# Seven products for eight in the first matmul of an fp32 MLP beside attention, with the second matmul's banks added to the output by transfers

## The chip, the core and the metric

The kernel runs on one core of a Trainium2 chip. The core has five engines with their own in-order instruction streams: TensorE (PE; matmuls from SBUF into PSUM), VectorE (DVE), ScalarE (ACT), GpSimd (POOL) and SyncE (SP, which mainly issues DMA transfers). They meet only at semaphores. The metric is the device time of one execution in microseconds; lower is better.

## What is computed

The input x is 2048 rows of 576 numbers in float32. It is normalised per row, and two branches take the result xn:

```
xn  = layernorm(x)
qkv = xn @ wqkv                      # 576 x 1728, 32 heads of 18
A   = softmax over 8 keys (positions s, s-2, ... s-14) of q.k, times v, then @ wo
B   = relu(xn @ w1) @ w2             # w1 576 x 4608, w2 4608 x 576
out = x + A + B
```

All is float32. Each large matmul is done with operands cut into a high and a low part (`hi` rounded to the matmul's fast float32 form, `lo` the rest), as hi*hi + hi*lo + lo*hi, so every product costs three matmuls on PE.

## The kernel before, in words

**Tiles.** Rows are taken in two phases (`ph`) of 1024 rows. A phase has 4 token blocks of 256 rows (`tb`), each of two tiles of 128 rows. F = 4608 is 36 tiles of 128 (`f`), in 12 chunks of 3. D = 576 is 4 K tiles of 128 and a rest of 64.

**Slots.** The main loop runs over slots, one for each phase, chunk, token block and F tile: 288 of them. In a slot the *second* product (`o_two`) multiplies the relu'd tile of that slot by w2 into four PSUM banks (two row tiles by the column halves 0:256 and 256:576), and the *first* product (`h_two`) makes two slots' tiles ahead, over two slots. After the third F tile of a chunk, `o_out` (line 765) adds the four banks to the running sum x in SBUF by DVE. After a phase's last chunk the sums are stored.

**Half rows.** Nearly all matmuls use 64 of the 128 rows of the array. `mm_rows` (line 137 of the profile) issues them in pairs, one on the lower and one on the upper 64 rows, which run together into different banks. A tile's first product is 27 such halves: 12 on the lower and 12 on the upper rows (3 hi/lo terms by 4 K tiles), and 3 for the 64 rest rows. Where a bank goes from lower to upper rows PE waits for the last matmul into it.

**First product's output.** ACT writes the high part with relu (line 651), DVE the low part (line 654).

**Attention.** Four units of 8 heads per phase. QKV for a unit runs in 8 slots; the attention itself is a list of DVE instructions (`bg`: multiply, reduce, softmax, multiply, add in halves) that `run_bg` pours into the gaps. It keeps an estimate of PE's and DVE's time (`t`) and lets DVE run at most a margin past PE. In chunk 10 the output projection wo joins the second product's banks; attention's output is turned to K-major either through PE (`turn_rows`, line 369) or by DVE's 32x32 transpose and a trip through DRAM (`blocks_out`, `words_in`).

**Weights.** SP loads tiles of w1, w2, wqkv, wo into staging buffers four tasks ahead; ACT makes `hi` (line 170) and DVE `lo` (line 174), POOL in the kernel's head (line 172).

Of the kernel before, what the change touches and what calls it, by code (L numbers as in the profile page):

```python
# [3 lines left out]

# [14 lines left out]
P = 128  # L19
# [7 lines left out]
C = 3  # L27
LAG = 2
ROW0 = 8
EPS = 1e-5  # L30

UNIT0, UNIT_STEP = (10, 10), 24
WO_CHUNK = 10


XT_STEPS = (
    (-6, -1, 0, 1, 2, 4, 6), (-5, 0, 2, 3, 4, 7, 8), (-3, 2, 4, 5, 6, 8, 9), (4, 6, 7, 10),
    (4, 6, 8, 12), (7, 9, 11, 13), (8, 12, 13, 15), (10, 13, 14, 16),
)

TURN_STEPS = ((-10, -9, -7, -4), (-7, -5, -3, -1), (-4, -3, 0, 1), (-2, 0, 1, 2))
WO_STEPS = (-2, -1)
# [13 lines left out]


@with_exitstack
def tile_body(ctx: ExitStack, tc: tile.TileContext, x, wqkv, wo, w1, w2, out):
# [6 lines left out]
    NCH = NF // C  # L66
# [7 lines left out]
    SPP = NCH * SPC  # L74
# [4 lines left out]

    def space(name, words):  # L80


        pool(name, 1).tile([P, words], F32, name=name)

    consts = pool("consts", 1)
    xp = pool("xp", 11)
    xtp = pool("xtp", NTB)
    qop = pool("qop", 1)
    kp = pool("kp", 1)
    vp = pool("vp", 2)  # L90
    w1p = pool("w1p", C + 1)
    space("gap_w2", 48)
    w2p = pool("w2p", C + 1)
    space("gap_wq", 16)
    wqp = pool("wqp", 1)
    stp = pool("stp", 5)
    hp = pool("hp", LAG + 1)
    prp = pool("prp", 2)
    lgp = pool("lgp", 1)
    smp = pool("smp", 2)  # L100
    space("gap_tmp", 16)
    tmp = pool("tmp", 2)
    turned = pool("turned", 4, space=bass.MemoryType.DRAM)
# [19 lines left out]

    t = {"pe": 0.0, "dve": 0.0}

# [3 lines left out]

    def mm_rows(runs, behind=None):  # L130


        if behind is not None:
            tc.add_manual_dep(nc.tensor.nop().ins, behind.ins.name, SYNC, reason="PSUM banks change rows")
        for pair in zip(*runs, strict=True):
            for z, (o, l, r, start, stop, n) in zip((slice(0, 64), slice(64, P)), pair):
                ins = nc.tensor.matmul(o, l[z], r[z], start=start, stop=stop)  # L137
            t["pe"] += pair[0][5] * 17 / 16 / 2400.0 + 0.001
        return ins

    def dve(n):
        t["dve"] += (n + 70) / 960.0

# [8 lines left out]
    def stage_more(ahead=None):  # L152
        while tasks and len(staged) < (ahead or AHEAD["n"]):
            step, load, split = tasks.popleft()
            st = stp.tile([P, 640], F32, name="st")
            load(st)
            staged.append((step, split, st))
# [11 lines left out]
    def two(hi, lo, src, n):  # L169
        nc.scalar.activation(hi, src, AF.Copy)  # L170
        if step_now in by_pool:
# [7 lines left out]
    def w1_task(step, key, f):  # L179
# [9 lines left out]
        def split(st):  # L189
            w = w1p.tile([P, 2, 5 * P], F32R, name="w1t")  # L190
            two(w[:, 0, :], w[:, 1, :], st[:, :], 640)
            W1[key] = w
# [3 lines left out]
    def w2_task(step, key, f):  # L196
# [3 lines left out]
        def split(st):  # L200
            w = w2p.tile([P, 2, 640], F32R, name="w2t")
            for z, c in zip(W2CUT, CUT):
                two(w[:, 0, z], w[:, 1, z], st[:, c], c.stop - c.start)
# [4 lines left out]
    def wq_tasks(steps, key, g):  # L208
        src = wqkv.rearrange("r (s c) -> r s c", s=3)

        def one(kt):
            def load(st):
                v = st[:, 0 : 3 * UD].rearrange("p (s c) -> p s c", s=3)
                c = slice(g * UD, (g + 1) * UD)
                if kt < KT:
                    nc.sync.dma_start(v, src[kt * P : (kt + 1) * P, :, c])
                else:
                    nc.sync.dma_start(v[0:DR], src[KT * P : D, :, c])
                    nc.sync.dma_start(v[DR:P], src[KT * P : D, :, c])

            def split(st):
                if kt == 0:
                    z = wqp.tile([P, WQ0 + 10 * WQS], F32R, name="wq")[:, WQ0:]
                    WQ[key] = z.rearrange("p (k c) -> p k c", c=WQS)[:, :, 0 : 3 * UD]
                w = WQ[key]
                two(w[:, kt, :], w[:, 5 + kt, :], st[:, 0 : 3 * UD], 3 * UD)

            return load, split

        for kt, step in enumerate(steps):  # L230
            split_task(step, *one(kt))

    def wo_tasks(steps, key):
        def one(kt):
            def load(st):
                if kt < KT:
                    nc.sync.dma_start(st[:, 0:D], wo[kt * P : (kt + 1) * P, :])
                else:
                    nc.sync.dma_start(st[0:DR, 0:D], wo[KT * P : D, :])
                    nc.sync.dma_start(st[DR:P, 0:D], wo[KT * P : D, :])  # L240

            def split(st):
                if kt == 0:
                    a = wqp.tile([P, 7, D], F32R, name="wq")
                    b = vp.tile([P, 3, D], F32R, name="v")
                    WO[key] = [a[:, k, :] for k in range(7)] + [b[:, k, :] for k in range(3)]
                w = WO[key]
                two(w[kt], w[5 + kt], st[:, 0:D], D)

            return load, split  # L250

        for kt, step in enumerate(steps):
            split_task(step, *one(kt))


    X, XT, XN, MR = {}, {}, {}, {}

    def load_x(ph, i):
        if (ph, i) not in X:
            X[ph, i] = xp.tile([P, D], F32, name="x")  # L260
# [7 lines left out]
    def stats(ph, i, parts=False, act=False):  # L268
        xt = X[ph, i]
# [22 lines left out]

    def norm(ph, i, act=False):
        nm, r = MR.pop((ph, i))
        xw = tmp.tile([P, 640], F32, name="xn", bufs=3)
        xn = xw[:, 0:D]
# [6 lines left out]
        if ph:  # L303
            nc.scalar.activation(xw[:, D:640], xn[:, KT * P : D], AF.Copy)
        XN[ph, i] = xw if ph else xn
# [35 lines left out]
    def make_xt(ph, i, bank=None, parts=False):  # L341
# [3 lines left out]
        d = XT[ph, tb][:, :, h * P : (h + 1) * P]  # L345
# [3 lines left out]
    def make_xt_rows(ph, i):  # L349
        tb, h = divmod(i, 2)  # L350
        if h == 0:
            XT[ph, tb] = xtp.tile([P, 10, TBN], F32R, name="xT")
        for c, pt in turn_rows(XN.pop((ph, i))):
            d = XT[ph, tb][:, :, h * P + c : h * P + c + 64]
            nc.scalar.activation(d[:, 5:10], pt, AF.Copy)
            nc.scalar.activation(d[0:DR, 4], pt[0:DR, KT], AF.Copy)
            nc.vector.tensor_tensor(d[:, 0:4], pt[:, 0:KT], f32(d[:, 5:9]), op=ALU.subtract)
            nc.vector.tensor_tensor(d[DR:P, 4], pt[DR:P, KT], f32(d[DR:P, 9]), op=ALU.subtract)
            dve(256)
            dve(64)  # L360

    def turn_rows(src):


        z = [(c, ps_m.tile([P, 5, 64], F32, name="pm")) for c in (0, 64)]
        for k in range(5):
            for c, pt in z:
                rows = slice(c, c + 64)
                nc.tensor.transpose(pt[:, k], src[rows, k * P : (k + 1) * P], ident[rows, rows])  # L369
        t["pe"] += 5 * 0.06  # L370
        return z

    def blocks_out(ph, i):
        td, tr = TD[ph, i]
        for r in range(4):
            rows = slice(32 * r, 32 * r + 32)
            nc.sync.dma_start(
                td[:, :, rows].rearrange("g j i -> j g i"),
                tr[rows, :].rearrange("j (g i) -> j g i", i=32),
# [606 lines left out]
```

## Time and profile before

| | |
|---|---|
| median of 2 runs | 1144.19 us (1143.83 to 1144.56) |
| span of the profiled execution | 1141.6 us; its time with what lies around the span is not listed apart, the median of the runs is 2.6 us over the span |
| PE busy | 1134.5 us, 99% of the span |
| DVE busy | 802.1 us, 70% |
| ACT busy | 303.0 us, 27% |
| POOL busy | 57.1 us, 5% |
| DMA | 83.60 MB, mean 73 GB/s |

The profile's page gives, per engine, the time in which it was executing, and then the chain of work that ended last: from the last instruction back, at each step, to what released it. Groups of instructions are listed as line, engine, operation, output<-inputs, shapes and count, then busy time and the mean of one, then the idle time of the engine just before them and what ended it. "64*128 64x256" on a matmul is 64 rows by 128 columns of weights with 256 moving columns. Matmuls overlap in the pipeline, so a single matmul's duration (273 ns) is longer than the distance from one pair to the next.

### The profile page before, as it was taken

How to read it: one execution, taken by the hardware profiler on the slowest of the kernel's cores; microseconds unless marked ns; L12 is line 12 of the kernel's file. 1: busy time of each engine (PE TensorE's matmuls, PEld its weight loads, DVE VectorE, ACT ScalarE, POOL GpSimd, SP SyncE). 2: the span in 40 equal slices, each digit the busy share in tenths (PEclk: the TensorE clock that was granted, in tenths of full speed). 3: DMA queues.
4: the chain of work that ended last, by engine and by line, in shares of the span. 5: the costliest groups of instructions: out<-in, count | busy, mean ns of one | idle time of the engine just before them, and what ended most of it. 6: DMA issues, size and time to landing. Idle time of an engine off the chain costs nothing.

```text
span 1141.6 us, 38695 instructions
## 1 busy us (share of the span) xinstructions
PE 1134.5 (99%) x17224; PEld 1128.4 (99%) x17224; DVE 802.1 (70%) x1522; ACT 303.0 (27%) x854; POOL 57.1 (5%) x84
## 2 busy tenths in 40 slices
PE   8999999999999999999999999999999999999998
PEld 8999999999999999999999999999999999999998
DVE  7415886887788689854674179868868887896433
ACT  4412222222232212322462122222222312222110
POOL 2400000000000000000110000000000000010000
PEclk9999999999999999999999999999999999999999
DMA  6303212130330312622633033032221304136002
GB/s 192 109 2 94 71 47 67 48 98 6 97 98 13 104 33 50 175 57 63 157 122 98 2 101 88 23 85 63 63 59 47 107 2 114 45 81 152 13 2 84
DMA packets 118855, 83.60 MB, mean 73 GB/s; under 512 B 33201, under 2 KB 102449, under 8 KB 118689
## 3 DMA queue, kind: packets, MB, share of 16 engines
q1 hardware_dynamic: 118256, 80.67, 25.6%
q8 instruction: 135, 2.21, 0.8%
q10 hardware_dynamic: 432, 0.46, 0.1%
q14 instruction: 32, 0.25, 0.1%
HBM read 64.95 MB, written 7.96 MB: 64 GB/s over the span
## 4 chain that ended last, share of the span: by engine, by line
PE 96%; issue 2%; DVE 1%; ACT 0%; DMA 0%; DVEq 0%; POOL 0%; ACTq 0%
PE po L137 41%; PE pm L137 28%; PE ph L137 24%; PE ph L127 1%; PE po L127 1%; PE pm L317 0%; DVE pr L544 0%; DMA x<-in_x 0%; PE pm L369 0%; DVE xn L613 0%; PE pm L127 0%; DVE hlo L654 0%; DVE x L765 0%; ACT xT L322 0%; DVE xn L614 0%
## 5 line engine op out<-in xcount | busy, mean ns | idle before, releaser
L137 PE MATMUL po<-w2t,hhi 64*128 64x256 f32 (+1 forms) x4448 | 444.8, 290 | 0.0
L137 PEld LDWEIGHTS po<-w2t,hhi 64*128 64x128 f32 x4448 | 356.1, 184 | 0.6
L137 PE MATMUL po<-w2t,hlo 64*128 64x256 f32 (+1 forms) x2224 | 331.2, 287 | 0.0
L137 PE MATMUL ph<-xT,w1t 64*128 64x256 f32 x4806 | 305.5, 273 | 0.3 <-DVE hlo L654 0.2
L137 PEld LDWEIGHTS ph<-xT,w1t 64*128 64x128 f32 x4806 | 293.7, 184 | 1.5 <-DVE hlo L654 1.1
L765 DVE TENSOR_TENSOR x<-po,x 128x320 f32<-128x320 f32 (+1 forms) x384 | 149.6, 449 | 149.4 <-PE po L137 146.8
L137 PEld LDWEIGHTS po<-w2t,hlo 64*128 64x128 f32 x2224 | 217.2, 184 | 0.0
L651 ACT ACTIVATE hhi<-ph 128x256 fp32r<-128x256 f32 x187 | 62.1, 382 | 496.8 <-PE ph L137 484.6
L137 PE MATMUL pm<-wq,xT 64*128 64x432 f32 x1728 | 178.8, 354 | 0.0
L137 PE MATMUL pm<-xT,w1t 64*128 64x256 f32 x2700 | 170.6, 273 | 0.0
L137 PEld LDWEIGHTS pm<-xT,w1t 64*128 64x128 f32 x2700 | 164.5, 184 | 0.0
L137 PEld LDWEIGHTS pm<-wq,xT 64*128 64x128 f32 x1728 | 160.0, 184 | 2.9
L654 DVE SCALAR_TENSOR_TENSOR hlo<-ph,hhi 128x256 fp32r<-128x256 f32 x187 | 70.8, 418 | 129.6 <-ACT hhi L651 129.5
L651 ACT ACTIVATE hhi<-pm 128x256 fp32r<-128x256 f32 x101 | 33.3, 381 | 214.1 <-PE pm L137 214.1
L505 DVE TENSOR_TENSOR pr<-qo,k 128x1152 f32<-128x1152 f32 x64 | 85.6, 1348 | 0.0
L508 DVE TENSOR_REDUCE lg<-pr 128x64 f32<-128x1152 f32 x64 | 85.3, 1342 | 0.0
L537 DVE TENSOR_TENSOR pr<-lg,v 128x1152 f32<-128x1152 f32 x64 | 85.0, 1348 | 0.3
L544 DVE TENSOR_TENSOR pr<-pr 128x288 f32<-128x288 f32 (+1 forms) x128 | 70.1, 600 | 0.1
L654 DVE SCALAR_TENSOR_TENSOR hlo<-pm,hhi 128x256 fp32r<-128x256 f32 x101 | 38.2, 418 | 32.9 <-ACT hhi L651 32.1
L170 ACT ACTIVATE w2t<-st 128x256 fp32r<-128x256 f32 (+1 forms) x144 | 56.3, 445 | 7.1 <-PE po L137 3.9
L174 DVE TENSOR_TENSOR w2t<-st,w2t 128x256 fp32r<-128x256 f32 (+1 forms) x142 | 57.9, 448 | 0.1
L174 DVE TENSOR_TENSOR w1t<-st,w1t 128x640 fp32r<-128x640 f32 x68 | 55.6, 817 | 2.4 <-ACT w1t L170 2.2
(99 smaller groups left out, 689.8 us busy)
## 6 DMA issues: line engine op xcount, KB each, us to landing
st<-in_w SPq DMA_DIRECT2D x72, 288.0 KB, 3.3
st<-in_w SPq DMA_DIRECT2D x72, 256.0 KB, 3.1
st<-in_wqkv SPq DMA_DIRECT2D x32, 216.0 KB, 3.0
st<-in_w SPq DMA_DIRECT2D x144, 32.0 KB, 2.8
out<-x SPq DMA_DIRECT2D x15, 288.0 KB, 2.4
x<-in_x SPq DMA_DIRECT2D x14, 288.0 KB, 4.4
k<-k SPq DMA_DIRECT2D x8, 441.0 KB, 3.9
v<-v SPq DMA_DIRECT2D x8, 441.0 KB, 4.7
```

What stands on the lines that cost most here:

```text
L127: nc.tensor.matmul(o, l, r, start=start, stop=stop)
L137: ins = nc.tensor.matmul(o, l[z], r[z], start=start, stop=stop)
L170: nc.scalar.activation(hi, src, AF.Copy)
L174: nc.vector.tensor_tensor(lo, src, f32(hi), op=ALU.subtract)
L505: nc.vector.tensor_tensor(pr[i], q, window(k, i), op=ALU.mult)
L508: nc.vector.tensor_reduce(lg[:, i], pr.pop(i).rearrange(heads, d=Dh), axis=AX.X, op=ALU.add)
L537: nc.vector.tensor_tensor(pr[i].rearrange(heads, d=Dh), e, window(v, i).rearrange(heads, d=Dh), op=ALU.mult)
L544: nc.vector.tensor_tensor(o, z[:, 0:n], z[:, n : 2 * n], op=ALU.add)
L651: nc.scalar.activation(hi, pt, AF.Relu)
L654: nc.vector.scalar_tensor_tensor(lo, pt, 0.0, f32(hi), op0=ALU.max, op1=ALU.subtract)
L765: nc.vector.tensor_tensor(acc[:, cols], PO[k, h], acc[:, cols], op=ALU.add)
```

## The change

Chunks 0 and 1 of each phase (6 F tiles) stay in the old slots. The other 30 F tiles are taken in 15 pairs, and the four token blocks in two pairs, which gives 30 *groups* per phase. In a group the first product over the 4 whole K tiles is a 2x2 block product: blocks of w1 by F tile (i) and K half (j), A11, A12, A21, A22; blocks of xn by K half and token block, B11, B12, B21, B22. It is done with seven block products for eight:

```
S1 = A21+A22   S2 = S1-A11   S3 = A11-A21   S4 = A12-S2
T1 = B12-B11   T2 = B22-T1   T3 = B22-B12   T4 = B21-T2
C11 = A11 B11 + A12 B21
q   = A11 B11 + S2 T2        r = q + S3 T3
C12 = q + S1 T1 + S4 B22     C21 = r + A22 T4     C22 = r + S1 T1
```

(each C also gets the 64 rest rows of K directly, `R`, as before). What sums, cuts and moves this needs:

- POOL makes S1 to S4 from staged w1 (`sw_mix`), ACT and DVE cut them into hi and lo (`sw_prep`); POOL makes the low half of w2 (`w2_prep`).
- T1 to T4 are made once per phase and token pair by DVE and ACT (`ts_steps`).
- Within PSUM: `seed` copies bank a to a new bank q, and q to r, by ACT (line 988), and matmuls go on adding there; `keep` copies a bank to SBUF (line 992) and `plus` adds another bank to it by DVE (line 997).
- `group` is written out by hand: 8 steps, each 6 pairs of first-product matmuls, then one half of a piece of the second product (6 pairs) for an earlier group. A piece is one column half of the output for two row tiles; four per group.
- The second product adds up over two F tiles, not three. Its banks go by ACT to one of four SBUF buffers (`evict`, line 717), and a DMA issued by POOL adds the buffer to the output in DRAM (line 721). The output starts as x plus the first chunk's banks (line 867); x is no longer kept in SBUF.
- QKV of units 1 to 3 moves into groups 4-5, 10-11 and 16-17. Attention's output goes to DRAM (line 610) and comes back for the output projection, which has PSUM banks of its own in a hand-written `epilogue`. All turns other than those of the kernel's head go by DVE and DRAM; the next phase's x is normalised and turned in groups 18 to 25.
- `run_bg`'s margins are new, and the planner's fixed cost of a DVE instruction is 150 cycles for 70.

The core of the diff:

```diff
+    def rows(lower, upper):
+        need = None
+        for z, run in enumerate((lower, upper)):
+            for e in run:
+                b = e[0]
+                if b.z is not None and b.z != z and b.seq > count["waited"] and (need is None or b.seq > need.seq):
+                    need = b
+        if need is not None:
+            tc.add_manual_dep(nc.tensor.nop().ins, need.ins.ins.name, SYNC, reason="PSUM banks change rows")
+            count["waited"] = need.seq
+        for pair in zip_longest(lower, upper):
...
+    def evict(ph, i, h, bank, what, by=None):
+        key = ph, i, what
+        if key not in EV:
+            EV[key] = evp.tile([P, D], F32, name="ev"), []
+        acc, done = EV[key]
+        cols = CUT[h]
+        nc.scalar.activation(acc[:, cols], bank, AF.Copy)
+        done.append(h)
+        if len(done) == 2:
+            del EV[key]
+            nc.gpsimd.dma_start(o_v[ph, i], acc, accum_op=ALU.add)
...
+    def sw_mix(k):
+        o, a, b, op = (
+            ("S1", "S3", "A22", ALU.add), ("S2", "S1", "A11", ALU.subtract),
+            ("S4", "A12", "S2", ALU.subtract), ("S3", "A11", "S3", ALU.subtract),
+        )[k]
+        nc.gpsimd.tensor_tensor(stg(o), stg(a), stg(b), op=op)
...
+    PROD = {
+        1: ("a", "A11", "B11"), 2: ("a", "A12", "B21"), 3: ("q", "S4", "B22"), 4: ("r", "A22", "T4"),
+        5: ("f", "S1", "T1"), 6: ("q", "S2", "T2"), 7: ("r", "S3", "T3"),
+    }
...
+    def seed(ph, g, to, src):
+        nc.scalar.activation(new_bank(ph, g, to).ap, B[ph, g, src].ap, AF.Copy)
+    def keep(ph, g, name, src):
+        z = PC[ph, g, name] = csp.tile([P, TBN], F32, name=name)
+        nc.scalar.activation(z, B[ph, g, src].ap, AF.Copy)
+    def plus(ph, g, name, src):
+        z = PC[ph, g, name]
+        t["dve"] = max(t["dve"], t["pe"] + 0.15)
+        nc.vector.tensor_tensor(z, z, B[ph, g, src].ap, op=ALU.add)
...
+        def step(i, lower, upper, after, early=()):
+            for name in early:
+                new_bank(ph, g, name)
+            rows(lower(), upper())
+            for f, *a in after:
+                f(*a)
+            fire(ph, g, i, "T")
+            run_bg(min(MARGIN, 0.7 + 1.4 * (8 - i) + 0.75))
+            og, piece = (g - 2, 2 + i // 2) if i < 4 else (g - 1, (i - 4) // 2)
+            if og >= 0:
+                o_half(ph, og, piece, i % 2 == 1)
+                if i % 2 == 1:
+                    o_evict(ph, og, piece)
+            for f, *a in late_after.get(i, ()):
+                f(*a)
+            fire(ph, g, i, "O")
+            for f, a in ins.pop((ph, g, i), ()):
+                f(*a)
+            run_bg(min(MARGIN, 0.7 + 1.4 * (8 - i)))
...
+        step(1, lambda: m(1, first=True), lambda: tail[0], [(plus, ph, prev, "m5", "q")], early="a")
+        step(2, lambda: tail[1], lambda: m(1, last=True), [(seed, ph, g, "q", "a")])
+        step(3, lambda: m(5, first=True), lambda: tail[2], [], early="f")
+        step(4, lambda: tail[3] + m(2)[0:3], lambda: m(6), [(lambda: c_parts(ph, prev, 1, 0, bank(ph, prev, "r")),)])
+        step(5, lambda: m(6, last=True), lambda: m(2), [(seed, ph, g, "r", "q")])
+        step(6, lambda: m(2, last=True)[3:] + R(ph, g, 0, 0), lambda: m(5, last=True), [
+            (keep, ph, g, "m5", "f"), (lambda: c_parts(ph, g, 0, 0, bank(ph, g, "a")),)])
+        step(7, lambda: m(3), lambda: m(7), [])
+        step(8, lambda: m(7, last=True), lambda: m(3)[0:3] + R(ph, g, 1, 1), [
+            (keep, ph, g, "u3", "r"), (plus, ph, g, "u3", "f")])
...
-            nc.vector.tensor_tensor(acc[:, cols], PO[k, h], acc[:, cols], op=ALU.add)
```

`M` lists the six matmuls of one product for one half of the rows (three hi/lo terms by two K tiles), `R` the three of the rest rows, `tail` holds what is left of the group before (product 3's second half, product 4, two rests).

1070 lines of the change are left out of this document (764 added, 306 removed).

## The prediction

> **What bounds the kernel now.** I read the page first: shares of the engines, clock, and the chain that ended last.
>
> ```profile
> span 1141.6 us, 38695 instructions
> PE 1134.5 (99%) x17224; PEld 1128.4 (99%) x17224; DVE 802.1 (70%) x1522; ACT 303.0 (27%) x854; POOL 57.1 (5%) x84
> PEclk9999999999999999999999999999999999999999
> PE 96%; issue 2%; DVE 1%; ACT 0%; DMA 0%; DVEq 0%; POOL 0%; ACTq 0%
> ```
>
> TensorE holds the chain for 96% and its clock is granted in full in all 40 slices. A busy PE need not be dense, so next comes the chain in order of time, in a plain stretch of two hidden blocks (200 us on):
>
> ```profile
> 201.45 1.59 PE ph L137 x28
> 203.05 1.55 PE po L137 x24
> 204.60 1.48 PE ph L137 x26
> 206.08 1.55 PE po L137 x24
> 207.63 1.59 PE pm L137 x28
> ```
>
> Nothing lies between the pieces. 54 matmuls are 27 pairs (lower and upper 64 rows run together) in 1.59 + 1.48 = 3.07 us: 0.114 us for a pair of 256 columns. One slot of the second product, 12 pairs, is 1.55. So the kernel is bound by the number of matmul pairs, and a pair taken away is worth its whole 0.114 us as long as nothing else becomes late. ACT with 27% and POOL with 5% have room; DVE with 70% has some.
>
> **What the change takes off PE.** Of the twelve chunks of F, ten per phase go to 30 groups; a group is 2 F tiles by 2 token blocks, four old slots. Before, four slots cost 2 x 3.07 = 6.14 us for the first product and 4 x 1.55 = 6.20 for the second. After, a group has 8 steps of 6 pairs, 48 for 54: 48/27 x 3.07 = 5.46. The second product keeps its 48 pairs. A group is then 11.66 us for 12.34; 60 groups give **-40.9**.
>
> The turns through PE go too: thirteen tiles (130 matmuls of 64 columns) now turn by DVE and DRAM. One tile, and the first matmul after it:
>
> ```profile
> 1070.02 0.50 PE L369 MATMUL pm<-ident,qo 64*128 64x64 f32 x10
> 1070.30 0.51 PE L137 MATMUL po<-w2t,hhi 64*128 64x256 f32 x4
> ```
>
> 0.28 us each by the starts, 13 x 0.28: **-3.6**. Against that, the first group of a phase and the epilogue leave 12 matmuls per phase without a partner: 24 half-used places, 24 x 0.057 = **+1.4**. QKV, output projection and the first 24 slots of each phase keep their pairs. The profiled execution's span is 1141.6, the median of the runs 1144.2, so 2.6 us lie outside the span and I keep them: 1144.2 - 40.9 - 3.6 + 1.4 = **1101.1** if everything added hides.
>
> **What is added, and what must hide it.** Durations by form (columns: line, engine, op, shapes, count | busy us, mean ns | idle before):
>
> ```profile
> L651 ACT ACTIVATE hhi<-ph 128x256 fp32r<-128x256 f32 x187 | 62.1, 382 | 496.8 <-PE ph L137 484.6 <-PE ph L127 12.2
> L612 ACT ACTIVATE k<-pm 128x320 fp32r<-128x320 f32 x16 | 6.2, 444 | 23.8 <-issue 23.8
> L170 ACT ACTIVATE w2t<-st 128x320 fp32r<-128x320 f32 x72 | 33.8, 469 | 0.0
> L414 ACT ACTIVATE xT<-xT 128x512 fp32r<-128x512 f32 x3 | 1.9, 628 | 1.7 <-DMA xT<-words 1.7
> L299 ACT ACTIVATE xn<-xn,rstd 128x576 f32<-128x576 f32 x7 | 5.4, 778 | 0.6
> ```
>
> *ACT.* A group gives it 4 relus, 2 seed copies from bank to bank, 2 copies to SBUF and 8 evictions (4 of 256, 4 of 320): 12 x 0.382 + 4 x 0.444 = 6.4 us; the splits of weights, per two groups, 4 of 256 (at 0.38), 2 of 320 and 3 of 512 columns, 1.5 + 0.9 + 1.9, half of it 2.2. Sum 8.6 of 11.66 us, 10.2 in groups 18 to 25 of phase 0 with two passes over x more. It holds, but ACT is in order and two copies sit on PE's path: the seed of bank q (issued after step 2, read in step 4) and of bank r (after 5, read in 7). A step is 11.66/8 = 1.46 us. Between the end of the rows of step 2 and those of step 4 lie two halves of the second product and one row block, about 2.2 us; ahead of the seed stand up to two evictions, a relu that waits for a DVE sum, and a split of 512, 0.76 + 0.38 + 0.63. So DVE may be late by about 1.4 us before PE waits.
>
> *DVE.* The 384 additions to x go, 32 stay; sums and turns come. Counting the changed program's instructions by these rows gives about 800 us, as before; what counts is where it is full. A group needs 4 low parts and 2 sums at 0.418 and 1.45 us of splits, 4.0 in all, and the planner fills the rest with attention.
>
> ```profile
> L654 DVE SCALAR_TENSOR_TENSOR hlo<-ph,hhi 128x256 fp32r<-128x256 f32 x187 | 70.8, 418 | 129.6 <-ACT hhi L651 129.5
> L505 DVE TENSOR_TENSOR pr<-qo,k 128x1152 f32<-128x1152 f32 x64 | 85.6, 1348 | 0.0
> L508 DVE TENSOR_REDUCE lg<-pr 128x64 f32<-128x1152 f32 x64 | 85.3, 1342 | 0.0
> L537 DVE TENSOR_TENSOR pr<-lg,v 128x1152 f32<-128x1152 f32 x64 | 85.0, 1348 | 0.3
> L544 DVE TENSOR_TENSOR pr<-pr 128x288 f32<-128x288 f32 (+1 forms) x128 | 70.1, 600 | 0.1
> L278 DVE BATCH_NORM_STATS2 bst<-x 128x6 f32<-128x288 f32 x32 | 12.9, 445 | 3.6 <-DMA x<-in_x 3.5
> L586 DVE STREAM_TRANSPOSE x<-qo 128x576 f32<-128x576 f32 x8 | 6.2, 770 | 0.0
> L599 DVE TENSOR_TENSOR xn<-xn,k 128x512 fp32r<-128x512 f32 x8 | 5.5, 689 | 2.8 <-ACT k L598 2.3
> ```
>
> A unit of attention is the first three of these and the sums, 326/8 = 41 us, and with its softmax and last sums some 47. In the order of the changed program the instructions of groups 6 to 10 (one unit of QKV in the last) make about 65.5 us of DVE in 68.9 of PE, 95%. Groups 18 to 25 of phase 0 hold nearly a whole unit (44 us), 48 low parts and sums (20.1), 25 splits (15), eight sets of statistics at about 1.25 (10) and seven turns (5.4): 95 in 93.3. There DVE has nothing to spare.
>
> *POOL* is new in the game: per two groups four sums of weights and four low halves of w2, and eight transfers that add to the output.
>
> ```profile
> L172 POOL TENSOR_TENSOR w2t<-st,w2t 128x256 fp32r<-128x256 f32 x1 | 0.7, 746 | 0.0
> L172 POOL TENSOR_TENSOR w2t<-st,w2t 128x320 fp32r<-128x320 f32 x1 | 0.9, 872 | 0.0
> L452 POOL MEMSET k<- 1x1008 f32 x8 | 7.5, 932 | 0.0
> ```
>
> 6 x 0.746 + 2 x 0.872 = 6.2 us of 23.3. No row shows a transfer issued by POOL: below, an issue as cheap as POOL's own small ops (0.2 us); above, some 3, if building the descriptors of 128 rows runs like three passes of the memset of 1008 words. I take 1.0, nearest to the memset, and keep both: 14 us of 23.3, hidden. The Trainium skill ("DMA: Bandwidth & Descriptors", Specifications) puts the first byte of a transfer from GpSimd at about 1 us, which would leave the sum as it is; no run here shows it yet.
>
> *Contention* is what I charge for. Two pairs of rows, a POOL op beside a DVE op, and what each takes alone (min/median/max):
>
> ```profile
> 32.01 1.11 POOL L172 TENSOR_TENSOR wq<-st,wq 128x432 fp32r<-128x432 f32 x1
> 32.08 1.35 DVE L301 TENSOR_SCALAR xn<-x,mv,rstd 128x576 f32<-128x576 f32 x1 [0.73 <-POOL rstd L285]
> ```
>
> ```profile
> L301 DVE TENSOR_SCALAR xn<-x,mv,rstd x6: 569/576/1354, 6.6 to 32.1; 128x576 f32<-128x576 f32 x6
> ```
>
> ```profile
> 449.01 1.35 DVE L537 TENSOR_TENSOR pr<-lg,v 128x1152 f32<-128x1152 f32 x1
> 449.01 1.44 POOL L546 COPY qo<-qo 128x64 f32<-128x64 f32 x1 [17.71 <-DVE qo L544]
> ```
>
> ```profile
> L546 POOL COPY qo<-qo x16: 231/533/1452, 449.0 to 1075.2; 128x64 f32<-128x64 f32 x16
> ```
>
> The DVE op lost 0.78 us to a POOL op of 1.11 that began just before it; the POOL copy of 0.23 waited out the whole DVE multiply. So each can block the other. The Trainium skill ("SBUF — State Buffer", Who interferes with whom) states it as a rule: a DVE instruction with two SBUF inputs and a GpSimd instruction that reads SBUF exclude each other, the later one waiting to the end; the rows agree for POOL behind DVE. That rule speaks against this change; what it would cost if every POOL op blocked DVE for its length is the first rival.
>
> In the stretches where attention fills DVE (groups 2-4, 6-10, 12-16 of both phases, 18-25 and 18-24) POOL's ops sum to 2 x (7.8 + 14.0 + 14.0) + 24.9 + 20.2 = 117 us by the counts above. Each stretch can lose what DVE has to spare in it (2.7, 3.4, 3.4 us; none; 3.7) plus the 1.4 us of lateness before PE notices. If DVE loses a quarter of POOL's time, only groups 18-25 overrun: 24.9/4 + 1.6 - 1.4 = 6 us. Below is 0; above, all of it, 85 us. I take **+5**, near the quarter: a POOL op that comes while DVE multiplies waits itself, and half of DVE's time is reduces or reads of PSUM.
>
> *Hand-overs.* The prologue puts two seeds between neighbours (0.38 and a signal each, about 1 us a phase), and the output projection now waits for attention through DRAM:
>
> ```profile
> out<-x SPq DMA_DIRECT2D x15, 288.0 KB, 2.4
> x<-in_x SPq DMA_DIRECT2D x14, 288.0 KB, 4.4
> words<-pr SPq DMA_DIRECT2D x12, 72.0 KB, 4.1
> xn<-words SPq DMA_DIRECT2D x8, 256.0 KB, 3.2
> ```
>
> In group 29 blocks go out after step 3, are fetched after step 6 (4.4 us for 4.1) and split from the end of step 8 (3.5 us for 3.2), with nothing ahead of the matmuls that want both tiles: about 1.7 us uncovered per phase, and again one wait in phase 1, whose second pair is split right before its use. Together 6 to 8; some like waits around the old projection go. **+6.** From below nothing, from above 15.
>
> An evicted row waits in one of four buffers, in two sets: a set is taken again six steps (8.7 us) after its transfer is issued. A transfer that adds must read and write the output: 2.4 to 6.8 us (store, or load and store in turn), so I cost it at nothing; past 8 us ACT stands, and with it the seeds. The volume:
>
> ```profile
> q1 hardware_dynamic: 118256, 80.67, 25.6%
> ```
>
> 268 additions of 288 KB move 79 MB and read as much; at this row's share per MB that is 50% of the 16 engines more, 75% in all: room, with later landings. SP's queue keeps its 288 loads of w1 and w2 and gains 52 block transfers, 32 writes of attention and their reads, several held by DVE; the weights behind them are issued about a group and a half ahead. The end stays as it is: the last 8 additions read the output back some 16 us after their last transfer was prepared.
>
> Sum: 1101.1 + 5 + 6 = **1112**, 2.8% under 1144.2. A measurement of this kernel can tell about 2% from no change: 1121.3 to 1167.1.
>
> **Rivals.** (a) DVE becomes the bound through POOL. At half of POOL's time lost: stretches of 14.0 lose 7.0 - 4.8 four times, 18-25 loses 12.6, 18-24 of phase 1 10.1 - 5.1: 27 us, 1128 + the hand-overs' spread: 1121 to 1150. For it: 95 us in 93.3; against it: DVE runs nearly empty (4 us a group) after each unit and can't be late for long. 0.17.
> (b) POOL's queue saturates, which ends slower. It decides at an issue of (23.3 - 6.2)/8 = 2.1 us: at 2.5, two groups take 26.2 for 23.3, PE waits for evicted buffers, 30 x 2.9 = 87 more: about 1199. Waits behind DVE's 1.35 us ops lower that point. Against it: the 0.93 us of the nearest row. 0.14.
> (c) The gain is made and lost: the seeds come late. 0.25 us at both seeds of 60 groups is 30 us: about 1142, no change. For it: ACT goes from 27% to about two thirds and in order; against: 2.2 us of room at each. 0.09.
> (d) Forecast, 1098 to 1121: 0.60.
>
> **Range and chances.** 1098 to 1152 takes in (d), (a), (c) and leaves (b) and a few hundredths out. Faster 0.62 (d and the edge of a), within 2% 0.22, slower 0.16.
>
> **What would show it.** 720 halves of 256 columns and the 130 turns gone from PE, and a group of 11.7 us in the chain in plain groups 26 to 28, where attention is over: if those are longer, it is (b) or (c), not (a). If (a), groups 18 to 25 are longer than 93 us, DVE ops with two SBUF inputs exceed their 1.348 and 0.689, and PE waits for the seeds behind DVE sums. If (b), the first wait of ACT's evictions is for a transfer and POOL is full. I am wrong if an issue costs over 2 us or an adding transfer over 8.

## The result, and the profile after

The changed kernel takes **1328.93 us** (1328.57 to 1329.30) for 1144.19: a ratio of 1.160, 95% interval 1.153 to 1.167. It is 16% slower, 185 us, and 228 us over the 1101.1 that the sum gave with everything added hidden. The page of the changed kernel, against the lines shown of before:

```profile
span 1326.8 us, 39041 instructions
PE 1165.7 (88%) x16410; PEld 1135.8 (86%) x16410; DVE 822.1 (62%) x1207; ACT 598.1 (45%) x1720; POOL 498.2 (38%) x574
PEclk9999999999999998996979999899999899999889
PE 49%; DMA 14%; issue 12%; DVE 10%; POOL 7%; ACT 4%; SPq 4%; POOLq 0%; DVEq 0%; ACTq 0%
```

PE has 814 matmuls less, near the 850 counted, but its share of the chain falls from 96% to 49%. DMA, DVE, POOL and SP's issues (SPq) stand in its place, each with a part; no engine but PE is over 62% busy.

A group's length can be read from ACT's copy of bank r to SBUF (`keep`, tile u), which comes once per group: group g lasts from copy g-1 to copy g. The rows group these copies: count, min/median/max ns, the first start and the last.

```profile
L992 ACT ACTIVATE u<-pm x7: 384/384/405, 1177.2 to 1248.3; 128x256 f32<-128x256 f32 x7
L992 ACT ACTIVATE u<-pm x9: 386/401/441, 416.0 to 553.0; 128x256 f32<-128x256 f32 x9
L992 ACT ACTIVATE u<-pm x3: 386/403/441, 139.2 to 182.3; 128x256 f32<-128x256 f32 x3
L992 ACT ACTIVATE u<-pm x2: 385/388/392, 600.8 to 797.4; 128x256 f32<-128x256 f32 x2
```

Seven copies in 71.1 us are 6 groups of 11.85; the last four of them take 11.7 each, as predicted. Groups 18 to 25 of phase 0 take 137.0 us (93.3 at 11.66). Groups 3 and 4 (staging of wqkv, then QKV) take 43.1. From the last group of phase 0 to the first of phase 1 pass 196.6. So the core of the change does what it should, and the loss lies where something else happens beside it.

How the load on the DMA engines has grown shows in the share that their 16 are busy. First a stretch of plain slots before; then, in the changed kernel, groups 18 to 25 of phase 0, the last plain groups of that phase, and what follows them (columns: us, busy of PE, PEld, DVE, ACT, POOL, granted clock, DMA share, GB/s):

```profile
200.00:224.00 24.00, 24.00 (x400) 24.00 (x398) 21.34 (x33) 5.13 (x14) 0.00 (x0) 1.00 0.18 44
```

```profile
416.00:553.00 137.00, 108.08 (x1558) 104.95 (x1556) 97.86 (x149) 70.85 (x188) 65.41 (x79) 0.90 0.82 160
577.00:601.00 24.00, 24.00 (x400) 24.00 (x398) 8.16 (x16) 13.87 (x41) 10.73 (x13) 1.00 0.94 157
601.00:622.00 21.00, 1.01 (x8) 0.52 (x6) 3.35 (x7) 3.68 (x9) 1.64 (x2) 0.59 0.85 196
```

The page's average is 71% (42.1 for the adding queue, 27.8 for the other, and little else); stages differ widely from it. The share alone makes no wait: at 0.94 PE runs dense, 11.7 us a group, while groups 18 to 25 lose 44 us at 0.82. A late landing costs time only where someone stands for it. In the last row PE does 1 us of work in 21. What it waits for stands in the queue of SP and in the waits of the changed kernel (engine, line waited for, sum, times, longest):

```profile
593.34 6.13 SPq L400 DMA_DIRECT2D words<-pr  x8
599.57 0.71 SPq L408 DMA_DIRECT2D xT<-words  x1
...
615.84 0.58 SPq L228 DMA_DIRECT2D st<-in_w  x1
616.47 0.43 SPq L408 DMA_DIRECT2D v<-words  x1
```

```profile
PE po L142 <- ACT v L680: 35.3, 4, 20.0
ACT wq L198 <- DMA st<-in_wqkv: 40.3, 18, 6.0
ACT pm L988 <- DVE ar L754: 91.0, 32, 5.2
PE ph L163 <- ACT pm L988: 21.5, 15, 5.3
PE ph L163 <- ACT ph L988: 9.0, 11, 1.2
PE po L163 <- POOL ar L200: 10.1, 9, 1.8
```

Eight block writes of attention's output take 6.1 us to issue. Behind them in the same in-order queue come 12 fetches of the next x and 10 weight loads, 0.5 to 0.7 us each for the most part, and only at 616.5 the fetch that PE's output projection needs. That is the 20 us. The second wait is a load of wqkv that lands after ACT asks for it; the third is the seed of bank r, which waits until DVE's low part has read the bank that it takes. The last three are PE's own: for the seeds of r and q, 30.5 us together, and for the low halves of w2 that POOL makes.

### The profile page after: what moved, and what is told of

Same layout as the page of the kernel before. It is cut to its first block, busy times and chain, and to the rows that moved or that the text cites. A ratio compares the mean times of both kernels' runs of the same rounds, so it can differ in the third digit from the quotient of the medians.

```text
span 1326.8 us, 39041 instructions
## 1 busy us (share of the span) xinstructions
PE 1165.7 (88%) x16410; PEld 1135.8 (86%) x16410; DVE 822.1 (62%) x1207; ACT 598.1 (45%) x1720; POOL 498.2 (38%) x574
## 3 DMA queue, kind: packets, MB, share of 16 engines
q0 software_dynamic: 38592, 79.05, 42.1%
q1 hardware_dynamic: 167456, 102.51, 27.8%
## 4 chain that ended last, share of the span: by engine, by line
PE 49%; DMA 14%; issue 12%; DVE 10%; POOL 7%; ACT 4%; SPq 4%; POOLq 0%; DVEq 0%; ACTq 0%
PE po L142 15%; PE po L163 12%; PE ph L163 6%; PE pm L163 5%; PE pm L142 4%; DMA st<-in_w 3%; PE ph L142 3%; POOL out L721 3%; DMA st<-in_wqkv 2%; DMA q<-in_x 2%; POOL ar L200 2%; SPq L400 2%; DVE ar L754 2%; POOL st L901 2%; DVE lg L569 2%
## 5 line engine op out<-in xcount | busy, mean ns | idle before, releaser
L163 PE MATMUL po<-ar 64*128 64x256 f32 (+1 forms) x5760 | 503.9, 296 | 15.8 <-POOL ar L200 10.1
L721 POOL DMA_DIRECT2D out<-ev x268 | 236.4, 1020 | 645.7 <-ACT ev L717 642.9
L163 PEld LDWEIGHTS po<-ar 64*128 64x128 f32 x5760 | 442.1, 190 | 20.9 <-POOL ar L200 12.4
L163 PE MATMUL ph<-xT,ar 64*128 64x256 f32 x2520 | 337.9, 285 | 25.7 <-ACT pm L988 21.5
L163 PEld LDWEIGHTS ph<-xT,ar 64*128 64x128 f32 x2520 | 299.9, 193 | 31.9 <-ACT pm L988 25.6
L717 ACT ACTIVATE ev<-po 128x320 f32<-128x320 f32 (+1 forms) x536 | 189.4, 408 | 203.1 <-PE po L163 136.6
L163 PE MATMUL pm<-xS,ar 64*128 64x256 f32 x2160 | 275.5, 281 | 2.0 <-DVE ar L754 1.3
L163 PEld LDWEIGHTS pm<-xS,ar 64*128 64x128 f32 x2160 | 248.3, 189 | 3.8 <-DVE ar L754 1.8
L200 POOL TENSOR_TENSOR ar<-st,ar 128x256 fp32r<-128x256 f32 (+2 forms) x124 | 143.2, 1159 | 101.0 <-ACT ar L198 92.1
L198 ACT ACTIVATE ar<-st 128x256 fp32r<-128x256 f32 (+3 forms) x304 | 153.5, 510 | 44.1 <-DMA st<-in_w 18.7
L569 DVE TENSOR_REDUCE lg<-pr 128x64 f32<-128x1152 f32 x64 | 85.3, 1343 | 0.0
L754 DVE SCALAR_TENSOR_TENSOR ar<-ph,ar 128x256 fp32r<-128x256 f32 x95 | 38.9, 421 | 73.7 <-ACT ar L750 72.2
```

What stands on the lines that cost most here:

```text
L163: b.ins = nc.tensor.matmul(b.ap, l[part], r[part], start=start, stop=stop, skip_group_check=skip)
L200: nc.gpsimd.tensor_tensor(lo, src, f32(hi), op=ALU.subtract)
L569: nc.vector.tensor_reduce(lg[:, i], pr.pop(i).rearrange(heads, d=Dh), axis=AX.X, op=ALU.add)
L717: nc.scalar.activation(acc[:, cols], bank, AF.Copy)
L721: nc.gpsimd.dma_start(o_v[ph, i], acc, accum_op=ALU.add)
L754: nc.vector.scalar_tensor_tensor(lo, src, 0.0, f32(hi), op0=ALU.max, op1=ALU.subtract)
```

## The experiments

My theory after the result was that three things wait in line: loads with too little lead, x's load in groups 18 to 25, and SP's order around the epilogue. The rival was one common limit, DVE with POOL beside it. Groups are numbered through both phases, so that 30 to 59 are those of phase 1.

Every variant was timed once, but for e4_all3, whose four times lie between 1288.2 and 1295.1 us. A difference of less than some 7 us between two variants is therefore not told from none.

### One order at a time, and all three

e1_feed, the staging of wqkv and wo:

```diff
-WO_PAIR = 11
+WO_PAIR = 13
...
-        feed = ((0, 0, 6, 1, 1), (0, 1, 1, 1, 4), (1, 1, 3, 1, 5), (0, 1, 4, 1, 7), (1, 1, 5, 1, 8))
+        feed = ((0, -2, 8, -1, 4), (1, -1, 3, -1, 7), (0, -1, 4, -1, 8), (0, 0, 6, 1, 3), (1, 1, 3, 1, 8))
```

> Only the staging of wqkv and wo is changed: the five loads of a unit are spread over four groups, each 4 to 5 steps (5.8 to 7.3 us) ahead of its split, for 2 to 3 steps; wo's go to groups 24 to 27. Theory (a landing of 3.9 to 5.5 us is not covered, ACT stands in order and PE behind it): groups 3, 9, 15, 33, 39, 45 fall from 18.4-19.9 to about 12 us, six times 7 = 42 us less, and wo's groups 52-53 some 6 more: 1329 to about 1282. Rival (these groups are long since ACT and DVE have too much to do there, through POOL's blocking or the splits themselves): the work only moves to other groups, under 12 us gained, 1317 or more.

Measured: 1310.2, 18.8 less. ACT's wait for wqkv falls from 40.3 us in 18 pieces to 4.2 in 3, yet groups 3, 9, 15 and their like in phase 1 stay at 15.4 to 16.8 us. Some two fifths of what they had over 11.7 was the landing; something else is behind the rest. Groups 18 to 25, which wo's staging now reaches, rise from 137.0 to 144.6 us.

e2_xq, x's load issued behind the four block writes of the tile before:

```diff
-                on(ph, g, 1, "T", xq_load, i)
+                if i == 0:
+                    on(ph, g, 1, "T", xq_load, i)
...
                 on(ph, g, 8, "O", blocks_out, 1, i)
+                if i + 1 < NI:
+                    on(ph, g, 8, "O", xq_load, i + 1)
```

> Only the load of the next phase's x is changed: it is issued behind the turn of the tile before, 4 steps earlier. Theory (DVE stands for a load that lands 5 to 7 us after its issue, with statistics queued in front of attention and the sums): groups 18 to 25 of phase 0 lose 2 to 4 us each, 137 us to about 115, in all 1329 to about 1307. Rival (DVE has too much to do in these groups, 95 us in my count and longer with POOL beside it): less than 8 us gained, 1321 or more.

Measured: 1321.9, 7.0 less, the rival's number, at the edge of what can be told. But the edit does not test the theory. SP's queue, the changed kernel first:

```profile
446.69 4.37 SPq L400 DMA_DIRECT2D words<-q  x4
451.15 1.44 SPq L415 DMA_DIRECT2D q<-in_x  x1
```

```profile
446.29 4.44 SPq L400 DMA_DIRECT2D words<-q  x4
450.82 1.78 SPq L415 DMA_DIRECT2D q<-in_x  x1
```

The load stood right behind the four block writes already, and my edit put it behind the same ones: it is issued 0.3 us sooner. Groups 18 to 25 take 134.5 us for 137.0.

e3_hand, attention's turns ahead of the epilogue (its loads, turns and block writes there fall away):

```diff
-        for i in range(2):
-            on(ph, last - 1, 8, "T", ot_load, ph, first + i)
-            on(ph, last, 2, "T", ot_turn, ph, first + i)
-            on(ph, last, 3, "O", blocks_out, ph, first + i)
...
+        for k in range(4):
+            for i in range(2 * WOB[ph][k], 2 * WOB[ph][k] + 2):
+                on(ph, last - 2 + k // 2, 1 + 4 * (k % 2), "T", ot_load, ph, i)
+                on(ph, last - 2 + k // 2, 4 + 4 * (k % 2), "T", ot_turn, ph, i)
+                on(ph, last - 2 + k // 2, 4 + 4 * (k % 2), "O", blocks_out, ph, i)
...
```

> Only attention's way to the output projection is changed: all eight tiles of a phase are loaded, turned and written to DRAM in groups 27 and 28, and the first two of four pairs fetched before the epilogue; the fetch of pair 0 stands ahead of the 12 fetches of the next x and the weight loads in SP's queue. Theory (SP's issue time and chained trips through DRAM make the epilogue wait): from u3 of group 29 to the next phase 197 us fall to about 145 and the end's 79 to about 45, 85 us less: about 1244. Rival (the epilogue waits for DVE or ACT work that is there in any order, or PE's lower clock): 30 us or less, 1299 or more.

Measured: 1318.0, 10.9 less, as little as the rival had. The hand-over fell from 196.6 to 160.1 and the end from 78.5 to 55, but groups 28 and 29 rose from 23.4 to 48 us in both phases: DVE, in order, now stands 8 to 9 us before each of three turns in phase 0 for a load that lies behind block writes. Most of the wait was moved, not removed.

e4_all3, the three together:

> The three edits together. Theory (three places of waiting that don't overlap): 42 + 22 + 85 = about 150 us less, 1329 to about 1180, still slower than before's 1144. Rival (one common limit, DVE with POOL beside it): the sum of the single gains is not reached by more than 30 us.

Measured: 1290.6, ratio to before 1.130 (1.127 to 1.133), 38.3 less; the single gains make 36.7. So they add up, which speaks against one common limit, but they are a quarter of what I expected.

### What lies beside them

e5 to e7 leave work out on top of e4_all3 (the core of each edit).

```diff
# e5_nopool
     def sw_mix(k):
+        return
...
-        two(w[:, 0, :], w[:, 1, :], st_new(i)[:, CUT[h]], CUT[h].stop - CUT[h].start, True)
+        nc.scalar.activation(w[:, 0, :], st_new(i)[:, CUT[h]], AF.Copy)
...
-                z.append([PP[g, piece, k], l[:, k * P : (k + 1) * P], w[:, b, :], False, False, False, n])
+                z.append([PP[g, piece, k], l[:, k * P : (k + 1) * P], w[:, 0, :], False, False, False, n])
...
# e6_noattn: the list of attention's DVE work is replaced by
         for i in range(0, NI, 2):
+            nc.sync.dma_start(OD[ph][i : i + 2, :, cols].rearrange("i p c -> p i c"), qo[:, i : i + 2, :])
...
# e7_plain
-            nc.gpsimd.dma_start(o_v[ph, i], acc, accum_op=ALU.add)
+            nc.gpsimd.dma_start(o_v[ph, i], acc)
```

> On top of the three edits together (1290.6 us). POOL's sums of w1 and its low halves of w2 are left out (the sums stay unmade, the second product uses the high half of w2 twice), so the result is not the reference's; POOL keeps its 268 transfers. Theory now (POOL and DVE shut each other out: rows of DVE's low part of 0.42 us at 2.44 beside three POOL sums): groups with attention lose 2 to 4 us each, about 60 us in all, 1290 to about 1230. Rival (waits for transfers and the in-order queues of ACT and SP): under 15 us gained, 1275 or more.

Measured: 1244.3, 46 less. Groups 3, 9, 15 come to 11.9 to 12.2 us, which the feed alone had not done; groups 18 to 25 do not change (138.1 in e4_all3, 137.6 here). That lies between theory and rival.

> On top of the three edits together. Attention's own DVE work is left out (queries are written to DRAM in place of its result, so the result is not the reference's); everything else stays. Theory (DVE late in the stretches of attention, with POOL's help): the six attention stretches and groups 18 to 25 come near 11.7 us a group, 100 us less, about 1190; what is left over 1101 is then SP's and the epilogues'. Rival (waits for transfers): 30 us or less.

Measured: 1249.5, 41 less and not 100. Even without attention's DVE work, groups 18 to 25 take 123.6 us. DVE's load is not the main thing. The 41 us and the 46 of e5_nopool overlap, since the work that is gone here is also work that POOL blocks.

> On top of the three edits together. The transfers of evicted rows overwrite the output and do not add to it (so the result is not the reference's): same count, same bytes sent, nothing read back. Theory (adding transfers cost nothing but their landing, which no one waits for): 1285 to 1290. Rival (their load on the 16 DMA engines makes every other landing late): landings fall by over 1 us and 25 us or more go, 1265 or less.

Measured: 1222.9, **68 less**, beyond the rival's number. I had held the adding transfers for harmless, since hardly anyone waits for them by name (ACT for a buffer: 17.3 us in e4_all3). Their load falls on all others: the writes of attention went from 4.5 to 1.9 us to land, the loads of weights from 4.5 and 5.4 to 3.7 and 3.6.

### More of SP's order

e8_order2: x's load ahead of the block writes, and attention's turns spread over groups 26 to 29.

```diff
                 on(ph, g, 8, "T", lambda i=i: turn(hold["xq"], 1, i))
+                if i + 1 < NI:
+                    on(ph, g, 8, "T", xq_load, i + 1)
```

> The three edits together, with two orders on SP mended: the next x tile is loaded ahead of the four block writes of the tile before (it stood behind them), and attention's turns are spread over groups 26 to 29, each pair loaded ahead of the block writes of the pair before. Theory (a queue of writes at 0.5 to 1 us each held up the loads): groups 28 and 29 fall from 27.6 and 20.9 to 13 in both phases, 45 us, and groups 18 to 25 lose 2 us each, 15 us: about 1230. Rival (DVE is too full for either): 1275 or more.

Measured: 1270.1, 20.5 less than e4_all3, for the 60 expected by the theory and 15 or less by the rival. Groups 28 and 29 fell by 20 us in phase 0, but group 27 rose from 12.7 to 23.8. Its queue and ACT's wait:

```profile
546.29 8.23 SPq L400 DMA_DIRECT2D words<-pr  x8
554.62 2.31 SPq L266 DMA_DIRECT2D st<-in_wo  x1
```

```profile
560.87 0.68 ACT L198 ACTIVATE wq<-st 128x576 fp32r<-128x576 f32 x1 [9.42 <-DMA st<-in_wo]
```

Eight block writes took 8.2 us to issue, a load of wo stood behind them, ACT stood 9.4 us for it, and with ACT the seeds.

e9_order3: w2's loads are issued ahead (`on(ph, a - 1, 6, "O", w2_raw, p, i)`, save where the buffers are taken), wo's groups are 22 to 25, x is turned in groups 21 to 28, attention's output in 27 to 29.

> Orders on SP mended further on top of the last (1270.1 us): w2's loads are issued ahead of the block writes of the group before, wo's loads lie in groups 22 to 25 ahead of attention's turns, the next x is turned in groups 21 to 28 (attention is nearly over there), attention's turns in 27 to 29. Theory (loads stand behind block writes in SP's queue, and ACT's splits behind the loads): groups 18 to 29 of phase 0 fall from 194 us to about 160, of phase 1 from 172 to about 155, about 1220. Rival (each place of waiting only makes room for the next, POOL's adding transfers keep all landings long): 1250 or more.

Measured: 1259.1, 11.0 less, which is the rival's number (1250 or more). Phase 0's groups 18 to 29 fell from 194 to 185 us only. All edits of this kind together take 69.8 us off the changed kernel. They change the order on SP, the lead of loads and the place of DVE's turns at once; of their parts only the feed (18.8 us) and an earlier form of attention's turns (10.9) were run alone.

e10_mixdve: the sums of w1 go to DVE (`nc.vector` for `nc.gpsimd` in `sw_mix`).

> As the run before, with the sums of w1 made by DVE for POOL (120 instructions). Theory (a run of three POOL sums shuts DVE out for 2.4 us in the middle of a chain from DVE by ACT to PE): odd groups 3, 9, 15 and 7, 13 of both phases fall to 12 to 12.5 us as they did with POOL's work left out, 30 us less than the run before, although DVE has 50 us more to do. Rival (DVE's load is the limit, whoever blocks it): as the run before or slower.

Measured: 1256.6, 2.5 less, which is no difference and so the rival's number. Groups 9 and 39 fell nearly as expected, from 15.4 and 16.4 to 12.8; groups 7 and 13 stayed at 14.0. In group 7 a DVE instruction takes 2.28 us for 0.42 beside a low half of w2, which POOL still makes here. Group 11 rose from 22.3 to 26.1 and group 41 likewise: DVE had the added work to do at a place where PE waits for it. So the theory holds in some groups, and what they gain is lost in others.

e11_allout: e9_order3 with the edits of e5_nopool and e7_plain.

> All three causes taken away together, on the orders of the two runs before: POOL's sums and low halves left out, and transfers that overwrite the output for those that add (the result is not the reference's). Theory (orders on SP, POOL beside DVE and the adding transfers' load are three causes that add up, and the step of 11.66 us a group was right): about 46 and 68 us less than the first of these runs, about 1110 to 1130, near the 1101 of the sum with nothing late. Rival (a fourth cause of like size, such as ACT's order or PE's clock): 1160 or more.

Measured: 1159.7, 99.4 less than e9_order3; the edits had taken 46 and 68 from e4_all3. Groups are now close to the step that I worked out: eleven copies over groups 18 to 27, and eight over plain groups of phase 1:

```profile
L993 ACT ACTIVATE u<-pm x11: 392/397/441, 381.1 to 503.9; 128x256 f32<-128x256 f32 x11
L993 ACT ACTIVATE u<-pm x8: 389/389/392, 1003.4 to 1086.8; 128x256 f32<-128x256 f32 x8
```

They are 12.3 and 11.9 us a group. But the time is the rival's (1160 or more) and not the theory's 1110 to 1130: 59 us over 1101 have at least one more cause.

### Each cause alone, on the changed kernel as it was

> The changed kernel with one edit: evicted rows overwrite the output and do not add to it (the result is not the reference's). In the reordered kernel this took 68 us off. Theory (the adding transfers fill the 16 DMA engines in the groups, 0.94 of them in groups 28 and 29, and every load and trip lands late; more is waited for here, where orders are worse): 70 to 100 us less than 1329, 1230 to 1260. Rival (the order on SP is what counts, and landings are late for it): 40 us or less, 1289 or more.

> The changed kernel with one edit: POOL's sums of w1 and low halves of w2 are left out (the result is not the reference's). It took 46 us off the reordered kernel. Theory (POOL and DVE shut each other out in the attention stretches, whatever the order on SP): 40 to 50 us less, about 1280 to 1289. Rival (in the changed kernel waits for loads hide it): under 20 us, 1309 or more.

> The changed kernel with both edits. What then stays over the 1101 of the sum is SP's order, staging and the trips through DRAM. Theory (three causes that add up): 1329 less the two single gains, within 15 us, about 1205; the reordered kernel with both had 1159.7, so order and trips are worth some 45 us here, against the 70 us they took off the changed kernel. Rival (the causes cover one another): both together gain 30 us less than the sum of the two.

Measured:

| | us | less than 1328.9 |
|---|---|---|
| e12_plain_alone: transfers that overwrite | 1262.7 | 66.3 |
| e13_nopool_alone: no sums and low halves on POOL | 1286.6 | 42.4 |
| e14_both_alone | 1227.2 | 101.7 |
| e9_order3: order, leads and turns alone | 1259.1 | 69.8 |
| e11_allout: these and both | 1159.7 | 169.2 |

12 falls a little short of its band and 13 is in it. 14 gives 101.7 for a sum of 108.7 (the 1205 expected supposed larger single gains), and the order edits are worth 69.8 with both costs there and 67.5 with both gone. So these are three causes that add up within some 9 us (178.5 as a sum, 169.2 together), and the rival of e14 falls.

The adding transfers in e12: the queue's row (packets, MB, share of the 16 engines) and the cost of an issue, the changed kernel first:

```profile
q0 software_dynamic: 38592, 79.05, 42.1%
L721 POOL DMA_DIRECT2D out<-ev x268 | 236.4, 1020 | 645.7 <-ACT ev L717 642.9
st<-in_w SPq DMA_DIRECT2D x120, 128.0 KB, 5.3
od<-q SPq DMA_DIRECT2D x32, 144.0 KB, 3.9
```

```profile
q0 software_dynamic: 21440, 79.05, 16.2%
L721 POOL DMA_DIRECT2D out<-ev x268 | 146.9, 550 | 659.1 <-ACT ev L717 653.1
st<-in_w SPq DMA_DIRECT2D x120, 128.0 KB, 3.5
od<-q SPq DMA_DIRECT2D x32, 144.0 KB, 1.9
401.00:521.00 120.00, 103.03 (x1530) 99.54 (x1529) 95.03 (x148) 69.43 (x187) 54.66 (x79) 0.96 0.62 179
544.00:568.00 24.00, 24.00 (x400) 24.00 (x398) 8.12 (x16) 13.87 (x41) 7.63 (x12) 1.00 0.46 145
```

The same 79 MB cost 0.421 x 1326.8 x 16 / 268 = 33.3 us of engine time for a transfer that adds and 0.162 x 1260.9 x 16 / 268 = 12.2 for one that overwrites. The DMA share falls from 0.94 to 0.46 in the plain groups and from 0.82 to 0.62 over groups 18 to 25, and most other transfers land sooner, most loads of weights by 0.4 to 1.8 us and attention's writes by 2.0. Groups 18 to 25 fall from 137.0 to 120.3, the hand-over from 196.6 to 186.5.

The edit also halves POOL's time for an issue (0.55 for 1.02 us), which would be another way to gain through POOL and DVE. e13 and e14 bound it: with POOL's sums and low halves gone DVE's low parts take 420 ns with either kind of transfer, and the edit still takes 59.3 of its 66.3 us (1286.6 to 1227.2).

POOL's blocking in e13, by the forms of DVE's low part and the multiplies, the changed kernel first:

```profile
L754 DVE SCALAR_TENSOR_TENSOR ar<-u,ar 128x256 fp32r<-128x256 f32 x60 | 45.0, 750 | 24.7 <-ACT ar L750 24.7
L754 DVE SCALAR_TENSOR_TENSOR ar<-ph,ar 128x256 fp32r<-128x256 f32 x95 | 38.9, 421 | 73.7 <-ACT ar L750 72.2
L601 DVE TENSOR_TENSOR pr<-lg,v 128x1152 f32<-128x1152 f32 x64 | 93.6, 1486 | 0.7
L569 DVE TENSOR_REDUCE lg<-pr 128x64 f32<-128x1152 f32 x64 | 85.3, 1343 | 0.0
```

```profile
L754 DVE SCALAR_TENSOR_TENSOR ar<-u,ar 128x256 fp32r<-128x256 f32 x60 | 25.2, 420 | 24.7 <-ACT ar L750 24.7
L754 DVE SCALAR_TENSOR_TENSOR ar<-ph,ar 128x256 fp32r<-128x256 f32 x95 | 39.1, 422 | 75.4 <-ACT ar L750 73.4
L601 DVE TENSOR_TENSOR pr<-lg,v 128x1152 f32<-128x1152 f32 x64 | 85.0, 1353 | 0.7
```

A low part that reads `u` from SBUF takes 750 ns in the changed kernel for 420 without POOL's work, while the same instruction that reads a PSUM bank takes 421 and 422. The reduce, too, keeps its length (1343 and 1345). One place in the changed kernel, DVE and POOL:

```profile
141.32 2.19 DVE L754 SCALAR_TENSOR_TENSOR ar<-u,ar 128x256 fp32r<-128x256 f32 x1 [0.48 <-ACT ar L750]
```

```profile
141.43 1.10 POOL L200 TENSOR_TENSOR ar<-st,ar 128x256 fp32r<-128x256 f32 x1
142.15 2.78 POOL L901 TENSOR_TENSOR st<-st 128x256 f32<-128x256 f32 x3
```

With POOL's work gone DVE's busy time falls from 822.1 to 749.6 us with the same 1207 instructions: 72.5 us of it was standing. The edit also takes away PE's 10.1 us of waits for POOL's low halves of w2, so not all of the 42 us need be DVE's. On e4_all3, where PE waits only 2.5 us for them, it still took 46.

## Why the prediction was wrong, point by point

**What bounds the kernel, and what leaves PE: right.** A plain group takes the 11.66 us that 48 pairs give. The -40.9 was made wherever nothing else was late; e11 shows it, within some tenths, over most groups.

**"75% in all: room, with later landings" failed, and is worth 66 us.** The step that failed is that I named the later landings and priced them at nothing. I asked who waits for the adding transfer (a buffer free within 8 us; it lands in 6.0) and not who waits for the transfers beside it: the two main loads of weights land in 4.7 and 5.3 us here, and in 3.9 and 3.5 in e12. Setting the load against the whole span hid this: the additions lie in the groups alone, where eight in 23.3 us at 33.3 / 16 give 71%, and the windows show 0.82 to 0.94 with the rest. The load itself came out right, 50% of 1141.6 or 571 us per engine against 42.1% of 1326.8 or 559, but partly by luck. The row that I took, 25.6% for 80.67 MB, gives 17.1 us for 288 KB, and I doubled it; measured are 12.2 without the addition and 2.7 times that with it. "Wrong if an adding transfer takes over 8 us" was the wrong sign to look for.

**"SP's queue keeps its 288 loads ... the end stays as it is" failed; the order edits against it are worth 68 to 70 us.** I counted the added issues and gave them no duration and no place in the queue. An issue takes 0.3 to 0.7 us for the most part, a block write up to 3.3, a turned tile has four writes and three fetches, and the queue is in order, so every block write that waits for DVE's turn holds the loads behind it. The end of the changed kernel has the same chain, by the chain of waits:

```profile
1245.01 0.87 SPq L400
1245.89 0.04 issue
1245.93 4.85 DMA words<-pr
...
1251.99 4.60 DMA v<-words
```

A pair of output tiles goes through it as issue, landing, issue, landing, and PE stands. "About 1.7 us uncovered per phase", and with it the "+6" for hand-overs, was worked out from landings alone. The hand-over of 196.6 us took 158 to 168 in the runs with the turns moved away, and in e11, at 158.2, PE stands only 10 us of it; the end fell from 78.5 to 56.8 us. Against e11 the term was some 60 us, and not 6, though part of that is the other causes.

**Contention "+5" was mis-sized: 42 us.** The mechanism was right, and so was the half of rival (a) that says DVE's ops with two SBUF inputs get longer and seeds wait behind DVE. Wrong were the place and the price. I charged groups 18 to 25, since DVE was full there, and they do not change without POOL's work (137.8 us in e13; only with the adding load gone too does it take 8 us there). The loss lies mostly in the odd groups, where POOL has its sums of w1 and two low halves of w2: group 7 falls from 13.6 to 11.7, group 3 from 19.3 to 16.5. I had costed the four low parts of a group at 0.418 from a row that reads PSUM; two of the four read SBUF, they are the ones that POOL blocks, and the low part that must free a bank for the seed is queued behind them on DVE. My lateness room of 1.4 us is less than one such wait (2.19 for 0.42). The Trainium skill ("SBUF — State Buffer", Who interferes with whom) states that, outside its two-port modes, a DVE instruction with at most one SBUF input does not contend with GpSimd, and that one with two contends with a GpSimd instruction that reads SBUF; the forms of L754 agree, 421 against 750 ns.

**Groups 18 to 25 "95 in 93.3": right as a count, wrong as the cause.** They took 137.0. Without the adding load they take 120.3, with POOL's work gone too 112.1, and with the order edits as well 12.3 us a group over groups 18 to 27. What I had not listed is that DVE stands in order before a load of x: 21.3 us of waits in the changed kernel, 8.6 in e12.

**Rivals.** (a) named a real mechanism at two thirds of its price. (b) did not happen: an issue takes 1.02 us, as taken, though the memset that I took it from does other work, so that the hit is luck. (c) did in part: PE waits 30.5 us for seeds, but those of r wait for DVE (91.0 us) and not for ACT's own work. None of the four held the adding transfers' load on the others, nor SP's order, so the range could not hold the time.

**What is left open.** With all three causes gone e11 is 59 us over 1101. Some 22 of them are in groups (58 groups take 826.5 us, where 46 of 11.66 and 12 of 22.3 with QKV make 804). PE stands 10 us in the hand-over and about 10 in the end and its drain, and the granted clock is 0.81 to 0.93 in 517 to 580 and 0.83 to 0.91 in 1101 to 1140 of that run. I did not separate what the trips through DRAM cost there from what the lower clock costs, so the cause of the rest stays open. Nor are the 69.8 us of the order edits split into order, lead and DVE's place. No version here beats the kernel before: the best that keep all the work are e10_mixdve with 1256.6 and e9_order3 with 1259.1.

## What to carry to other kernels

Price a new transfer by what it does to the landings of all others in the stretch where it runs, not by its own landing and not by a share over the whole span. Give every DMA issue a duration and a place in its in-order queue, and ask which load stands behind an issue that waits for an engine. When a row gives the price of an instruction, check that its operands lie in the same memory, for here POOL's work blocked the one form and left the other alone.

## What the runs showed of the hardware

A 288 KB transfer that adds to DRAM took 2.7 times the DMA engine time of one that overwrites (33.3 against 12.2 us over 16 engines), 6.0 against 3.2 us to land, 144 packets against 80, and 1.02 against 0.55 us of POOL's time to issue. In the changed kernel a DMA issue on SP took 0.35 to 0.6 us in the median for a weight load, by line, and 0.53 and 0.71 for the writes of 128-byte pieces, with single ones up to 3.3. The granted clock of PE was lower where PE stood: 1.00 in the last plain groups of phase 0, 0.59 in the 21 us of waiting after them, and 0.74 to 0.91 in stretches to 700 us in which PE was busy for 57 of 78 us.
